# A transformer block on one core: the first queries and keys projected in parts, dense products in single pieces

## The chip, the cores and the metric

The kernel runs on one core of a Trainium2 chip. The metric is the device time of one execution in microseconds (us). Five engines work side by side, each on its own list of instructions, and wait for one another by semaphores: PE (matrix products, weights loaded beside them as PEld), DVE (vector), ACT (scalar functions), POOL (GpSimd) and SP, which here only issues DMAs. ACT can issue DMAs too. In a profile, L749 is line 749 of the kernel.

## The reference

```python
x = A_x                                     # 1 x 2048 x 512, bf16
h = x + attention(layernorm(x))             # 32 heads of 16; softmax over 2048 keys, then @ wo
h2 = h + (gelu(n @ w_gate) * (n @ w_up)) @ w_down     # n = layernorm(h); F = 1792
```

The scores of a head are (q . k) / 4; their softmax takes the maximum over all 2048 keys before the exponential.

## The kernel before, in words

**Scheduling.** The kernel is written by a planner in Python (class `Plan`). It keeps a clock for each engine, guesses when each operand is ready (`SEM`: a semaphore's delay; `pe_at`: the gap when PE changes its mode; `mm`: a product's length), and writes the instructions out in the order that its main loop finds. Only the order and the waits reach the chip; the guesses don't.

**Units and rows.** The 2048 queries are cut into 12 groups (four of 256, eight of 128), the 32 heads into 8 slots of four heads. A unit is one group with one slot: 96 units. A unit's first pass takes the row maxima: for each 512 keys, each 128 queries and each pair of heads, PE writes two banks of scores (L746) and DVE reduces them (L749, 128 x 1024 values). That is a "row"; there are 1024. Two pairs of banks alternate, so PE can be two rows ahead of DVE. Partial maxima are joined on POOL (L783, L784), or by a small reduction on DVE in the 128-wide groups (L808), split in three bf16 parts (L800 to L803), turned by a transposing DMA on SP (L823) and added to the queries on POOL (L828) in spare rows of the head's 32.

The second pass computes scores transposed, keys on partitions (L895), with the maximum already subtracted; ACT takes the exponential of 512 columns at a time (L904; 2048 of them, 32 for a unit of 256 queries, 16 for one of 128) into 34 tiles named PTM, PTE and PTG. PE multiplies them with the values (L926, a ones column giving the sums). Then come normalising (L960), the output projection, the second layer norm and the gated layer: gate and up (L1143), down (L1171), with GELU steps on POOL and ACT.

**PE's modes.** Scores are "rows" in the planner (32-row tiles of the array, mode `r`). All else is "dense": pieces of 0.22 us in the planner's clock, four to an item such as a projection, up to 56 products for a part of the gated layer. A change between the two waits for the products under way. The main loop picks a row or a dense piece. Coming from rows it may turn to dense work if ACT has enough queued (`LATE`) or the banks are not free; once there, it goes on while `nd`, the time spent since, is under 0.43, or while the piece would end ahead of both deadlines `D1` (DVE's) and `D2` (ACT's). Where PE would be idle, it multiplies a tile of ones (L452, "dummy") so that the array stays busy; `WARM` is the activity of the last 2.8 us under which that is forced.

**The head.** SP loads four x tiles of 128 tokens one by one (L470), then x tiles 4 to 7 (L473), the key weights and the query weights (L477), x tiles 8 to 11 and 12 to 15, the value weights, and wo (L484), each of 512 KB. DVE takes each tile's mean and variance (`ln_stats`, L503 and L504) and adds eps (L507), POOL the inverse root (L508), DVE normalises (`ln_norm`, L511), PE transposes (L538), ACT copies out (L540). After four tiles PE projects all 512 keys of the first chunk and then all 512 queries (L646) of the first 128 columns; ACT writes the keys (L675), DVE the queries (L671). A slot holds heads shifted by 16 partitions: odd slots come from a copy QKS (ACT, L680), moved by a DMA from SP (L687) into one of two QKS2 buffers and masked on POOL (L659). The statistics of tiles 4 to 7 are DVE's, ahead of the first row, and their normalising is POOL's (`ln_chain`, L521 to L531). Tiles 8 to 15 have their sums taken on ACT (`late_stats`, L1387), two passes a tile, and are normalised on POOL.

**Queues.** The first 32 rows belong to units 0 and 1 in an order by chunks of keys, and can be exchanged when keys are late. Key projections of the later chunks and the transposes stand in a list served first (`prio`); the other projections stand behind (`ready_q`), and both need a free QKS and QKS2 buffer (`can_projT`). POOL's work is a list with priorities (`jobs`), ACT's extra work another (`act_jobs`).

Of the kernel before, what the change touches and what calls it, by code (L numbers as in the profile page):

```python
# [19 lines left out]
class Plan:  # L20

    ENGINES = ("pe", "act", "dve", "pool", "sp")
    SEM = 0.045
    INF = float("inf")
# [118 lines left out]
    def pe_at(self, mode, tile=0, dep=0.0):  # L143
        t = max(dep, self.pe_last + 0.004)
        if self.pe_mode is not None and mode != self.pe_mode:
            return max(t, self.pe_drain + 0.09)
        return max(t, self.pe_tile.get(tile, 0.0))

    def mm(self, fn, reads=(), writes=(), n=512, mode="f", tile=0, sig=False, slow=1, extra=()):
# [8 lines left out]
        run = slow * n / (2400.0 if t > 4.8 else 1200.0) + 0.0025  # L158
# [103 lines left out]
def bass_sequential_preLN__mha_block__geglu_ffn__prompt_kernel(nc, A_x, A_wqkv, A_wo, B_x, B_w_gate, B_w_up, B_w_down, out):  # L262
    with ExitStack() as es:
# [175 lines left out]
        def run_act_jobs(now, force=False):  # L439
# [3 lines left out]
            for k, (fn, reads, writes) in enumerate(act_jobs):  # L443
                r = P.ready("act", reads, writes)
                if r <= max(a.free, now) + 0.02 and ((a.free <= now + 0.9) if force else (exps[0] - last_extra[0] >= 2)):
# [30 lines left out]
        def load_w(i, nm, lat):  # L476
            P.dma("sp", lambda e: e.dma_start(out=wqkv_sb[:, :, i * D:i * D + D], in_=wv[:, :, i * D:i * D + D]), nm, writes=[nm], lat=lat)  # L477
# [24 lines left out]
        def ln_stats(t):  # L502
            dve(lambda e: e.bn_stats(out=stats[:, t, :], in_=x_sb[:, t, :]), [("x", t)], [("stats", t)], 0.694, 0.672)  # L503
            dve(lambda e: e.bn_aggr(out=mv[:, t, :], in_=stats[:, t, :]), [("stats", t)], [("mv", t)], 0.1, 0.193)  # L504
# [5 lines left out]
        def ln_norm(t):  # L510
            dve(lambda e: e.tensor_scalar(out=xn_sb[:, t, :], in0=x_sb[:, t, :], scalar1=mv[:, t, 0:1], scalar2=rstd[:, t:t + 1], op0=ALU.subtract, op1=ALU.mult),  # L511
                [("x", t), ("rstd", t), ("mv", t)], [("xn", t)], 0.33, 0.43)

        def ln_chain(c, have_mv):
# [15 lines left out]
            for t in ts:  # L530
                ops.append(o(lambda e, t=t: e.tensor_scalar(out=xn_sb[:, t, :], in0=x_sb[:, t, :], scalar1=rstd[:, t:t + 1], scalar2=nmr1[:, t:t + 1], op0=ALU.mult, op1=ALU.add),  # L531
# [74 lines left out]
        def qkv_finished():  # L606
            qkv_over[0] = True
            fk = [("xnT", t) for t in range(NT)] + ["wk", "wq", "wv"] + [("QKS", i_) for i_ in range(4)] + [("QKS2", i_) for i_ in range(2)]
# [23 lines left out]
        def can_projT(it):  # L632
            return not (qks_busy.get(("a", qk_n[0] % 4)) or qks_busy.get(("b", qk_n[0] % 2)))

        def item_projT(it, which, ht, c):
            nm = "w" + which
# [17 lines left out]
            def mask(src, key, slot, bk):  # L654
# [9 lines left out]
                jobs.add(1, [(fn, [key, "qmask", "kmask", "kbias", "zero1"], keys, 0.74, 0.78, ())], then=over)  # L664
# [70 lines left out]
        def p1_issue():  # L735
# [18 lines left out]
            p1_on[0] = True  # L754
            nq = nq_of(gi)
# [252 lines left out]
        def add_ffn(gi):  # L1008
# [4 lines left out]
            fs = [list(range(a, min(NFC, a + nf))) for a in range(0, NFC, nf)]  # L1013
            for f, fcs in enumerate(fs):
                add_item(item_gate, gi, f, fcs, can=lambda i_, f=f: not par_busy[f % 2])
                add_item(item_up, gi, f, fcs)
            for k in range(nq_of(gi)):
                add_item(item_down, gi, k, can=lambda i_: not gut_left.get(gi, 0))
# [343 lines left out]
        for t in range(4):  # L1362
# [3 lines left out]
        def run_now(fn, b, *a):  # L1366
            it = Item(fn, a)
            it.b = b
            it.begin()
            try:  # L1370
                while True:
                    fill(P.ready("pe", it.req[1]), 7)
                    it.req = next(it.gen)
            except StopIteration:
                pass
# [204 lines left out]
```

## Time and profile before

| what | value |
|---|---|
| median of 3 runs | 1245.37 us |
| lowest, highest | 1240.93, 1245.42 us |
| the profiled execution's own time | 1243.96 us |
| its span, first to last instruction | 1242.2 us |
| mean granted TensorE clock | 0.990 |
| DVE busy, ACT busy, PE busy | 1194.4, 1196.1, 1170.5 us |
| POOL busy | 802.3 us |
| first row's maximum starts | 13.61 us |
| last row's maximum starts | 1203.05 us |

The profile is of one execution; times in it count from the span's start. A group's line gives the source line, the engine and operation, what it writes and reads, how many there are, then the busy time in us and the mean of one in ns, then the engine's idle time just ahead of them and what ended most of it. In a timeline row the first two numbers are the start and the length (merged rows cover several instructions), and the bracket gives the idle time before it and who ended it. In a table by stage, the stretch comes first, then its length, each engine's busy time and count, the granted clock and the DMA share. Busy time counts overlapping instructions once, so an engine with pipelined instructions can be busy throughout and still have room: for that the distance from start to start is the better measure.

### The profile page before, as it was taken

How to read it: one execution, taken by the hardware profiler on the slowest of the kernel's cores; microseconds unless marked ns; L12 is line 12 of the kernel's file. 1: busy time of each engine (PE TensorE's matmuls, PEld its weight loads, DVE VectorE, ACT ScalarE, POOL GpSimd, SP SyncE). 2: the span in 40 equal slices, each digit the busy share in tenths (PEclk: the TensorE clock that was granted, in tenths of full speed). 3: DMA queues.
4: the chain of work that ended last, by engine and by line, in shares of the span. 5: the costliest groups of instructions: out<-in, count | busy, mean ns of one | idle time of the engine just before them, and what ended most of it. 6: DMA issues, size and time to landing. Idle time of an engine off the chain costs nothing.

```text
span 1242.2 us, 39638 instructions
## 1 busy us (share of the span) xinstructions
PE 1170.5 (94%) x16858; PEld 612.4 (49%) x16997; DVE 1194.4 (96%) x1145; ACT 1196.1 (96%) x2503; POOL 802.3 (65%) x1629
## 2 busy tenths in 40 slices
PE   9999999999999999999999999999999999999998
PEld 5333333344334443334355655565656565666566
DVE  7999999999999999999999999999999999999982
ACT  6699999999999999999999999999999999999995
POOL 7667533778546984678826787394948484768254
PEclk9999999999999999999999999999989998999999
DMA  5011410000011000100000000100000000010000
GB/s 158 24 36 35 142 61 22 14 6 4 10 27 12 6 6 12 27 11 5 5 22 20 18 10 7 22 11 20 10 18 6 15 15 14 11 18 6 19 15 10
DMA packets 52081, 28.25 MB, mean 23 GB/s; under 512 B 37184, under 2 KB 50880, under 8 KB 51904
## 3 DMA queue, kind: packets, MB, share of 16 engines
q1 hardware_dynamic: 51904, 25.71, 8.3%
q8 instruction: 133, 2.18, 0.7%
q14 instruction: 44, 0.36, 0.1%
HBM read 11.80 MB, written 2.10 MB: 11 GB/s over the span
## 4 chain that ended last, share of the span: by engine, by line
ACT 59%; PE 19%; DVE 16%; POOL 3%; issue 1%; DMA 1%; POOLq 0%; DVEq 0%; ACTq 0%
ACT PTM L904 36%; DVE PM L749 16%; ACT PTG L904 10%; ACT PTE L904 6%; PE pbank L895 5%; PE pbank L746 3%; PE pbank L926 2%; PE pbank L1171 2%; PE pbank L452 2%; ACT th_sb L1124 1%; PE pbank L646 1%; PE pbank L697 1%; ACT g_sb L576 1%; ACT u_sb L576 1%; ACT OA L576 1%
## 5 line engine op out<-in xcount | busy, mean ns | idle before, releaser
L749 DVE TENSOR_REDUCE PM<-pbank 128x2 f32<-128x1024 f32 x1024 | 1173.4, 1221 | 17.1 <-PE pbank L746 7.0
L904 ACT ACTIVATE PTM<-pbank 128x512 bf16<-128x512 f32 x1388 | 730.1, 669 | 7.2 <-PE pbank L895 4.6
L895 PE MATMUL pbank<-QT,KT 32*128 32x128 bf16 (+1 forms) x6144 | 607.0, 236 | 23.5 <-ACT PTM L904 3.0
L746 PE MATMUL pbank<-KT,QT 32*128 32x512 bf16 x2048 | 398.9, 387 | 18.4 <-DVE PM L749 9.2
L895 PEld LDWEIGHTS pbank<-QT,KT 32*128 32x128 bf16 x6144 | 302.9, 93 | 228.2 <-issue 77.6
L904 ACT ACTIVATE PTG<-pbank 128x512 bf16<-128x512 f32 x420 | 225.8, 656 | 1.9 <-PE pbank L895 1.2
L746 PEld LDWEIGHTS pbank<-KT,QT 32*128 32x128 bf16 x2048 | 96.6, 91 | 175.5 <-DVE PM L749 83.6
L452 PE MATMUL pbank<-ones_bf 128*128 128x512 bf16 (+1 forms) x499 | 143.8, 365 | 13.3 <-issue 3.9
L926 PE MATMUL pbank<-PTM,VA 128*17 128x128 bf16 (+1 forms) x4164 | 135.1, 240 | 2.4 <-ACT PTM L904 0.8
L904 ACT ACTIVATE PTE<-pbank 128x512 bf16<-128x512 f32 x240 | 133.3, 656 | 1.4 <-PE pbank L895 1.3
L960 POOL TENSOR_TENSOR LINV<-OAT,negone 128x4 f32<-128x4 f32 (+1 forms) x94 | 114.9, 1232 | 28.9 <-ACT OAT L576 27.7
L926 PEld LDWEIGHTS pbank<-PTM,VA 128*17 128x17 bf16 x4164 | 78.2, 91 | 35.4 <-issue 15.1
L828 POOL TENSOR_TENSOR QT<-QT,STG 128x128 bf16<-128x128 bf16 (+1 forms) x95 | 48.2, 508 | 54.4 <-DMA STG<-ST 53.7
L800 POOL CAST ST<-NEGM 128x4 bf16<-128x4 f32 (+1 forms) x95 | 19.7, 207 | 94.5 <-DVE NEGM L808 92.0
L452 PEld LDWEIGHTS pbank<-ones_bf 128*128 128x128 bf16 x585 | 43.8, 98 | 71.9 <-ACT PTM L904 25.9
L783 POOL TENSOR_TENSOR MX<-PM,MX 128x8 f32<-128x8 f32 x96 | 19.4, 202 | 87.1 <-DVE PM L749 84.1
L1143 PE MATMUL pbank<-hnT_l,wg_sb 128*128 128x128 bf16 (+1 forms) x616 | 67.7, 241 | 1.1 <-ACT PTM L904 0.4
L1143 PE MATMUL pbank<-hnT_l,wu_sb 128*128 128x128 bf16 (+1 forms) x616 | 68.3, 240 | 0.4 <-ACT PTM L904 0.2
L1126 POOL TENSOR_TENSOR th_sb<-th_sb,g_sb 128x512 f32<-128x512 f32 (+1 forms) x56 | 67.1, 1199 | 1.5
L1130 POOL TENSOR_TENSOR th_sb<-th_sb,g_sb 128x512 f32<-128x512 f32 (+1 forms) x56 | 67.1, 1200 | 1.3
L1114 POOL TENSOR_TENSOR GUT<-th_sb,u_sb 128x512 bf16<-128x512 f32 (+1 forms) x56 | 66.9, 1200 | 1.4
L1171 PE MATMUL pbank<-wd_sb,GUT 128*128 128x512 bf16 (+1 forms) x214 | 62.3, 379 | 3.4 <-issue 2.4
(146 smaller groups left out, 1113.1 us busy)
## 6 DMA issues: line engine op xcount, KB each, us to landing
QKS<-QKS SPq DMA_DIRECT2D x32, 112.0 KB, 2.2
xres<-in_A_x_dram SPq DMA_DIRECT2D x16, 128.0 KB, 2.3
out_dram<-out_sb SPq DMA_DIRECT2D x15, 128.0 KB, 1.7
wg_sb<-in_B_w_gate_dram SPq DMA_DIRECT2D x4, 448.0 KB, 5.6
wu_sb<-in_B_w_up_dram SPq DMA_DIRECT2D x4, 448.0 KB, 7.3
x_sb<-in_A_x_dram SPq DMA_DIRECT2D x3, 512.0 KB, 7.1
wqkv_sb<-in_A_wqkv_dram SPq DMA_DIRECT2D x3, 512.0 KB, 6.2
STG<-ST SPq DMA_TRANSPOSE x96, 2.3
```

The costliest lines, as they stand in the source:

```text
L452: P.mm(lambda e: e.matmul(pbank[:, b, 0:n], ones_bf[:, 0:128], ones_bf[:, 0:n], start=True, stop=True), reads=["ones_bf"], writes=[("pb", ...
L746: P.mm(lambda e, g=g, b=b0 + jj: e.matmul(pbank[:, b, :], QT[32 * g:32 * g + 32, c, slot, col:col + 128], KT[32 * g:32 * g + 32, slot, 512 ...
L749: dve(lambda e: e.tensor_reduce(out=PM[:, par, kc, qh, 2 * gp:2 * gp + 2], in_=pbank[:, b0:b0 + 2, :], axis=AX.X, op=ALU.max), [("pb", b0) ...
L895: P.mm(lambda e, kt=kt, i=i: e.matmul(pbank[:, b, w * i:w * i + w], KT[32 * g:32 * g + 32, slot, 128 * kt:128 * kt + 128], QT[32 * g:32 * ...
L904: act(lambda e: e.activation(out=PTt(pi), in_=pbank[:, b, :], func=ACT.Exp), [("pb", b)], [("PT", pi)], 512, lat=0.605, ivl=0.48, extra=dX)
L926: P.mm(lambda e, g=g, kt=kt, pi=pi, i=i: e.matmul(pbank[32 * g:32 * g + 17, b, 0:w], VA[:, kt, head(slot, g), :], PTt(pi)[:, w * i:w * i + ...
L960: inv = [((lambda e, a=a: e.tensor_tensor(out=LINV[:, par, a:a + hh], in0=oat[:, a:a + hh, 16], in1=negone[:, 0:hh], op=ALU.pow)), [("OAT" ...
L1114: jobs.add(3, [o(lambda e: e.tensor_tensor(out=o_ap, in0=shp(ts_), in1=shp(us), op=ALU.mult), [kt, ku], [("GUT", fc) for fc in fcs], 1.25, ...
L1126: o(lambda e: e.tensor_tensor(out=ts_, in0=ts_, in1=gs, op=ALU.mult), [kt, kg], [kt], 1.25)], then=second)
L1130: o(lambda e: e.tensor_tensor(out=ts_, in0=ts_, in1=gs, op=ALU.mult), [kt, kg], [kt], 1.25)], then=first)
L1143: P.mm(lambda e, dc=dc, fc=fc, i=i: e.matmul(pbank[:, it.b, w * i:w * i + w], wsb[:, dc, 128 * fc:128 * fc + 128], hT[:, dc, 0:w], start=( ...
L1171: P.mm(lambda e: e.matmul(pbank[:, b, 0:cols[1] - cols[0]], GUT[:, fc, 128 * k:128 * k + 128], wd_sb[:, fc, cols[0]:cols[1]], start=(fc == ...
```

## The change

- Planner's constants: a semaphore's delay, the gap at a change of mode and the length of products are set longer.
- The first 128 columns of the query and key weights are loaded by two DMAs of their own on ACT's queue, at the start; SP loads x tiles 4 to 15, then the value weights, then the rest of the key and query weights.
- Head: DVE takes the statistics of tiles 0 to 3 in a row; ACT normalises tiles 0 and 1 (POOL makes the product of mean and inverse root), DVE tiles 2 and 3. 256 queries are projected after two tiles and copied by DVE; 384 keys after three tiles (copied by ACT), the last 128 keys after the fourth (by DVE). The other 256 queries follow. Copies for the shift are taken in parts.
- Statistics of tile 4 and 5 stay ahead of the first row; tiles 6 and 7 have theirs after rows 0 and 1, and are normalised by DVE after rows 4 and 5 (`DNORM`); POOL normalises 4 and 5.
- Before the exponentials start, up to three ACT jobs can be placed in one turn of the main loop, with a shorter look ahead; values may be projected while up to four ACT jobs are left; other projections wait until no key projection of the first columns is left in `prio`; an item of low priority can be paused for one of high priority.
- Main loop: after one piece (`nd` under 0.2) PE goes back to rows unless the next piece ends ahead of both deadlines; from row 881 on the limit is 0.43 as before. Thresholds: WARM 1.7 (1.6), LATE 1.0 (1.1), 1.30 (1.20), ACT's margin in D2 0.47 (0.40), the margin of the next piece 0.1 (0.09).
- Items of the gated layer get a pacing test, `paced`, with PACEG = 0.

The core of the diff:

```diff
-    SEM = 0.045
+    SEM = 0.048
...
-            return max(t, self.pe_drain + 0.09)
+            return max(t, self.pe_drain + (0.096 if mode == "r" else 0.091))
...
-        run = slow * n / (2400.0 if t > 4.8 else 1200.0) + 0.0025
+        run = slow * n / (2400.0 if t > 4.8 else 1200.0) + (0.011 if mode == "r" else 0.008 if n >= 512 else 0.004)
...
+        load_w(0, "wq0", 4.0, 0, 128, "act")
+        load_w(1, "wk0", 4.3, 0, 128, "act")
         load_x(1, 4.1)
-        load_w(1, "wk", 5.1)
-        load_w(0, "wq", 6.1)
-        load_x(2, 7.1)
-        load_x(3, 8.1)
-        load_w(2, "wv", 9.1)
+        load_x(2, 5.1)
+        load_x(3, 6.1)
+        load_w(2, "wv", 7.1)
+        load_w(1, "wk", 7.9, 128, D)
+        load_w(0, "wq", 8.7, 128, D)
...
         def can_projT(it):
+            if it.args[:2] != ("k", 0) and any(i_.fn is item_projT for i_ in prio):
+                return False
...
-                jobs.add(1, [(fn, [key, "qmask", "kmask", "kbias", "zero1"], keys, 0.74, 0.78, ())], then=over)
+                jobs.add(1 if ht == 0 and which == "k" else 2, [(fn, [key, "qmask", "kmask", "kbias", "zero1"], keys, 0.74, 0.78, ())], then=over)
...
+            def paced(j):
+                return gi >= PACEG or p1_i[0] >= n0 + rows * j / tot or P.warmth(max(P.pe_last, clock[0]), 2.8) < COOL
...
+        PACE, PACEG, COOL = 0.7, 0, 1.7
...
-        ln_stats(0)
-        ln_rstd(0)
-        ln_stats(1)
-        ln_rstd(1)
         for t in range(4):
+            ln_stats(t)
+            ln_rstd(t)
+            if t < 2:
+                ln_nmr(t)
+        ln_norm_act(0)
+        ln_norm_act(1)
+        for t in (2, 3):
             ln_norm(t)
-            if t < 2:
-                ln_stats(t + 2)
-                ln_rstd(t + 2)
-        for t in range(4, 8):
-            ln_stats(t)
+        ln_stats(4)
...
-        run_now(item_projT, 4, "k", 0, 0)
-        run_now(item_projT, 5, "q", 0, 0)
-        ln_chain(1, True)
...
+        head_T(0)
+        head_T(1)
+        head_T(2)
+        head_mm("q", 6, 0, 256)
+        t_q = head_q(6, 0, 256, "dve")
+        ln_stats(5)
+        head_T(3)
+        head_mm("k", 4, 0, 384)
...
+        head_mm("k", 5, 384, 512)
...
+        head_mm("q", 7, 256, 512)
+        head_qks(0, 6, 0, 256, [t_q])
+        head_qks(1, 4, 0, 384)
+        tok = head_qks(1, 5, 384, 512, [t_k])
...
+        head_q(7, 256, 512, "act")
...
+        dve_stats(1, (0, 1))
+        for t, r in DNORM.items():
+            row_hooks.setdefault(r, []).append(lambda t=t: ln_norm(t))
...
-        WARM, HOT, LATE = 1.6, 0.8, 1.1
+        WARM, HOT, LATE = 1.7, 0.8, 1.0
...
-            D2 = max(f2, a_eng.free - 0.40)
+            D2 = max(f2, a_eng.free - 0.47)
...
-                if sd < INF and sd <= best_row + 0.4 and (nd < 0.43 or ed + 0.09 <= min(D1, D2)):
+                if sd < INF and sd <= best_row + 0.4 and (nd < (0.43 if p1_i[0] > 880 else 0.2) or ed + 0.1 <= min(D1, D2)):
```

The new functions, in short: `ln_norm_act` normalises on ACT (scale = inverse root, bias = -mean times it, made by `ln_nmr` on POOL), `head_T` transposes a tile and has ACT copy it out, `head_mm` projects a range of tokens by four products, `head_q` copies queries on DVE or ACT, `head_qks` takes the copy for the shift, `head_shift` issues it on SP and masks on POOL, `dve_stats` puts statistics on DVE after given rows.

More of the change, by code (lines that the diff above doesn't have):

```diff
@@ L754, in p1_issue @@
             p1_on[0] = True
+            for fn_ in row_hooks.pop(n, ()):
+                fn_()
             nq = nq_of(gi)
@@ new lines, in head_q @@
+        def head_q(b, c0, c1, eng):
+            keys = [("qT", 0, t) for t in range(c0 // 128, c1 // 128)]
+            if eng == "dve":
+                return dve(lambda e: e.tensor_scalar(out=QT[:, 0, 0, c0:c1], in0=pbank[:, b, 0:c1 - c0], scalar1=qmask[:, 0:1], scalar2=None, op0=ALU.mult), [("pb", b), "qmask"], keys, 0.33, 0.43)
+            else:
+                act(lambda e: e.activation(out=QT[:, 0, 0, c0:c1], in_=pbank[:, b, 0:c1 - c0], func=ACT.Copy, scale=qmask[:, 0:1]), [("pb", b), "qmask"], keys, c1 - c0, lat=0.5, ivl=0.4)
@@ new lines, in head_qks, with head_shift, over @@
+        def head_qks(si, b, c0, c1, extra=()):
+            keys = [("QKSp", si, c0)] + ([("QKS", si)] if c1 == 512 else [])
+            return act(lambda e: e.activation(out=QKS[:, si, c0:c1], in_=pbank[:, b, 0:c1 - c0], func=ACT.Copy), [("pb", b)], keys, c1 - c0, extra=extra)
+        def head_shift(si, c0, o_ap, keys, s1, s2_):
+            P.dma("sp", lambda e: e.dma_start(out=QKS2[0:112, si, :], in_=QKS[16:128, si, :]), ("qks", si), reads=[("QKS", si), ("QKSp", si, 0), ("QKSp", si, c0)], writes=[("QKS2", si)], lat=2.2)
+            def over(t):
+                qks_busy[("a", si)] = qks_busy[("b", si)] = False
+                qkv_check()
+            jobs.add(1, [(lambda e: e.tensor_scalar(out=o_ap, in0=QKS2[:, si, :], scalar1=s1[:, 0:1], scalar2=s2_[:, 0:1], op0=ALU.mult, op1=ALU.add),
+                          [("QKS2", si), "qmask", "kmask", "kbias", "zero1"], keys, 0.74, 0.78, ())], then=over)
```

104 lines of the change are left out of this document (73 added, 31 removed).

## The prediction

> **What bounds the kernel now.** I read the engine sums first, then the costliest groups, then the sums by stage, then the timeline of the first 60 us.
>
> ```profile
> PE 1170.5 (94%) x16858; PEld 612.4 (49%) x16997; DVE 1194.4 (96%) x1145; ACT 1196.1 (96%) x2503; POOL 802.3 (65%) x1629
> ...
> L749 DVE TENSOR_REDUCE PM<-pbank 128x2 f32<-128x1024 f32 x1024 | 1173.4, 1221 | 17.1 <-PE pbank L746 7.0
> L904 ACT ACTIVATE PTM<-pbank 128x512 bf16<-128x512 f32 x1388 | 730.1, 669 | 7.2 <-PE pbank L895 4.6
> ...
> L452 PE MATMUL pbank<-ones_bf 128*128 128x512 bf16 (+1 forms) x499 | 143.8, 365 | 13.3 <-issue 3.9
> ```
>
> Three engines look full, but not alike. The maxima ("rows", L749) start every 1.131 us when nothing holds them up (the median from start to start), so 1024 take 1158.1 us. The exponentials (L904) start every 0.478 us, and with every other ACT operation at its own usual spacing ACT needs some 1090 of the 1145 us from 60 to 1205. PE holds 143.8 us of filler matmuls (L452). So DVE is the bound and ACT follows it with about 5% to spare. Counting rows against exponentials agrees: two exponentials belong to a row, and ACT is 70 behind at 100 us, 50 at 600, 33 at 1200, which is about one unit of work: it has caught up and waits for rows. The time is therefore: start of the first row + 1158.1 + what DVE loses between rows + what follows the last row.
>
> ```profile
> core 0: us, PE busy (x) PEld busy (x) DVE busy (x) ACT busy (x) POOL busy (x), PEclk, DMA share, GB/s
> 12.00:60.00 48.00, 46.89 (x302) 20.95 (x304) 41.62 (x38) 34.58 (x77) 35.74 (x78) 1.00 0.17 51
> 60.00:1038.00 978.00, 924.32 (x13065) 461.62 (x13178) 971.37 (x895) 969.35 (x2022) 647.44 (x1332) 0.99 0.08 20
> 1038.00:1204.00 166.00, 156.34 (x2905) 101.51 (x2927) 161.67 (x157) 163.07 (x351) 95.05 (x181) 0.98 0.06 13
> 1204.00:1242.20 38.20, 32.29 (x559) 23.52 (x550) 11.09 (x31) 24.82 (x51) 18.76 (x23) 0.95 0.06 13
> ```
>
> DVE is idle mostly in the head. By the starts of rows: row 0 at 13.61, row 32 at 55.73, row 880 at 1033.06, the last at 1203.05. Less 1.131 a row, and 0.087 (start to start) for each of the small maxima of the 128-wide groups, DVE loses **5.9** us up to row 32, **14.2** up to row 880, **6.7** after it. The last row ends at 1204.28, and 37.9 us of tail follow.
>
> ```profile
> 8.46 0.41 DVE L511 TENSOR_SCALAR xn_sb<-x_sb,mv,rstd 128x512 bf16<-128x512 bf16 x1 [0.44 <-POOL rstd L508]
> ...
> 11.42 0.78 ACT L675 ACTIVATE KT<-pbank,kbias,kmask 128x512 bf16<-128x512 f32 x1 [1.21 <-PE pbank L646]
> ...
> 12.28 0.75 DVE L671 TENSOR_SCALAR QT<-pbank,qmask 128x512 bf16<-128x512 f32 x1 [0.21 <-PE pbank L646]
> ...
> 13.61 4.62 DVE L749 TENSOR_REDUCE PM<-pbank 128x2 f32<-128x1024 f32 x4 [0.57 <-PE pbank L746]
> ...
> 19.28 4.62 DVE L749 TENSOR_REDUCE PM<-pbank 128x2 f32<-128x1024 f32 x4 [1.05 <-PE pbank L746]
> ```
>
> The first row waits for a chain: fourth tile normalised, transposed, all 512 keys projected, all 512 queries projected, queries copied out. Then the rows starve four times (1.05, 1.14, 2.54, 0.51 us) because keys come late.
>
> **The head, step by step.** (a) Statistics of tiles 0 to 3 follow each other at the 1.01 us seen between the first two (2.93, 3.94): tile 3 starts at 5.96 instead of 6.60. Its inverse root on POOL (0.65) ends near 7.8, also behind the two small new POOL products (0.25 each), so its normalising starts at 7.9 instead of 8.46. (b) Tiles 0 and 1 go to ACT (nearest row: the 0.62 of L1387, same shape from SBUF), near 5.1 and 6.1, and their copies of transposes queue behind; that is done by 7.9, before tile 2's. (c) 256 queries: projected near 8.0 to 8.5, copied out by DVE behind the statistics of tile 4 (8.3 to 9.1), so at 9.1 to 9.5, then tile 5 until 10.35. (d) Tile 3 transposed at 8.4, out of PSUM at 9.5; 384 keys projected beside that, out on ACT at 9.55 to 10.2; the last 128 keys projected by 9.9 and copied by DVE behind tile 5 at 10.35 to 10.55. The first row's matmul took 0.43 to its maximum (13.18, 13.61): first row at **11.1**.
>
> Loads: two new 128-column pieces of weights go out on ACT's queue (SP's issues take 0.40 to 0.51 each, so ACT's table load moves from 0.78 to about 1.7, and ACT is first needed at 5.1). They bring 256 KB ahead of or among the four x tiles, which landed at 2.90, 3.30, 3.94, 4.39 against uses at 2.93, 3.94, 5, 6. Bounds: nothing (they land behind) and 0.75 (a later 512 KB load took 1.5 us from landing to landing). I take 0.2, because only tile 0 has no slack: first row at **11.3, so -2.3** (-2.7 to -1.6). The big loads keep their sum on SP, x before weights, which helps. [...]
>
> (e) Added between rows: statistics of tiles 6 and 7 (0.80 each, the spacing of 8.79, 9.60) and two normalisings (0.41 each): **+2.4** on DVE, nothing hides them unless DVE would idle. What is queued behind them is the next row. (f) Starving: the second unit's keys and queries start their shift over SP near 11.8 instead of 12.7, and POOL isn't busy with four 0.77 us normalisings when they land, so row 4 isn't late: -1.05. Rows 4 to 7 end at 22.8 with the additions; tile 7 normalised at 20.5, transposed and copied by 21.7, second 512 keys out by 23.7, so row 8 at 24.1: 1.35 idle (before 1.14). Afterwards the key projections no longer queue behind other projections holding the shift buffers (before, such a projection ran at 17.23 and the keys waited until 22.35), and the later statistics are taken into ACT earlier: of 2.54 + 0.51 I leave 1.0. With 0.15 for small gaps 2.5 stays of 5.9: **-3.4** (0 to -5). Cover that can fail: weights for the second quarter now land last and start after the keys, near 35 us; unit 2 needs them at row 32, 52 us. Head in sum: -2.3 + 2.4 - 3.4 = **-3.3**; row 32 at 52.4.
>
> **Single pieces and new constants.** Out of row mode, PE may now issue one 0.22 us piece, and a second only if DVE's and ACT's backlog allow it, up to row 880; before, two were always allowed. In the trace, 852 such visits lie between 60 and 1204 us: 163 under 0.40 us (one piece, typically 0.32), 488 of 0.40 to 0.62 (two, 0.54), 201 longer. The row delays right behind them sum to 0.6, 9.1 and 6.3 us, with 3.5 behind none. So 79% of the 14.2 us up to row 880, 11.2 us, comes from long visits, and a short visit costs 0.0035 against 0.022. DVE has up to two rows in its two bank pairs when PE leaves, so I let half of the second pieces stay: 11.2 x 0.5 x 0.84 = **-4.7** (bounds -11.2, and a loss, the slower rival). The planner's new latencies, thresholds and the wider ACT margin only order the work; no row prices them: 0, bounds 5 either way (the waits at half clock, below). The pacing test is true for every group (its limit is group 0): nothing. After row 880 two pieces stay allowed, and the tail has its old code: 0.
>
> Sum: 1243.96 - 3.3 - 4.7 = **1236.0** by the profiled execution (span 1242.2 and 1.8 around it). The runs have the median 1245.37 and go from 1240.93, so the profiled one lies between them; I keep 1236.0.
>
> **Rivals.**
> - *Head only* (1240.7): DVE's waits come from the meeting of three engines and not from the length of a visit; -3.3 stays and the middle doesn't move. For it: 3.5 us lie behind no visit, and 4.9 of the waits stand in stretches at half clock. Against: the steep ratio of 0.022 to 0.0035.
> - *Nearly all goes* (1226.5): -3.3, all 11.2 and, by the planner's better latencies, a third of the last 6.7. For it: the waits are short (19 for L895, the longest 0.8), such as a planner errs by.
> - *PE runs out of room* (1254.7, slower). A split pair costs 0.64 instead of 0.54, and up to 0.1 more for the way in (0.15 to 0.21 from the last row matmul's start). About 560 pairs stand before row 880. Half split at 0.15 is 42 us, and the fillers there (111.5 us) cover that even if only every second one is movable. From about 75% split at 0.2 it is 84 us against 56: up to 28 short, then the products of exponentials and values fall behind, the 34 exponential tiles stay full, and ACT and then DVE stop. Half of 28, since second pieces return when nothing else is ready: 1243.96 - 3.3 + 14. Against: a third of the visits up to 600 us are fillers alone.
> - *No effect in sum* (1244): the head's lead is eaten by row 32 (late weights), the second pieces are nearly always allowed.
>
> The clock bears on all of them. It is halved in five stretches from 204 to 1044 us (20.5 us in all), in which DVE loses 4.9, although PE is busy 3.5 to 4.0 of 4 us there. So the raised filler threshold may remove up to 4.9, and shorter visits may add as much; I take 0. [...]
>
> **Numbers.** Forecast 0.40 (own range 1230 to 1240); head only 0.22; nearly all 0.18; PE 0.17; no effect 0.03. About 0.5%, 6.2 us, is what a measurement can tell from no change: under 1239.1 is faster, over 1251.6 slower. Faster 0.36 + 0.18 = 0.54, same 0.04 + 0.22 + 0.03 = 0.29, slower 0.17. Range 1222 to 1255: from the second rival less the constants' bound to the third.
>
> **What would show it.** First row at 11.3; gaps of rows after 8 and 12; row 32 at 52.4; loss up to row 880 near 9.5; fewer visits over 0.4 us and fewer L452. Wrong if the first row comes after 12, if row 32 lies past 54.5, or if ACT shows long waits for L895 between 300 and 1000 us.

## The result and the profile after

| | before | after |
|---|---|---|
| median of 11 runs each | 1241.79 us | 1261.51 us |
| lowest, highest | 1239.55, 1245.42 | 1248.26, 1273.18 |
| ratio, 95% interval | | 1.0116 [1.0085, 1.0146] |
| the profiled execution | 1243.96 | 1261.51 |
| its span, mean granted clock | 1242.2, 0.990 | 1259.8, 0.970 |
| row 0, row 32 | 13.61, 55.73 | 13.34, 55.36 |
| row 880, last row | 1033.06, 1203.05 | 1044.92, 1208.28 |
| from the last row's start to the end | 39.2 | 51.5 |

The change made the kernel slower. The ratios, here and below, leave out runs over 1.5% above the fastest of the same kernel (four of the eleven after); by their clock these belong with the rest, so the medians, 1.6% apart here, say more than the ratio. The spans differ by 17.6 us: -0.3 at row 0, -0.1 from there to row 32, **+12.2 from row 32 to row 880**, -6.6 from there to the last row, **+12.3 in the tail**. The last two belong together, as will be seen: from row 880 to the end the change takes 5.7 us more.

The profile's page after, engine sums, granted clock by slices of 31.5 us, and three groups (line 766 holds the maxima, 914 the transposed scores, 923 the exponentials):

```profile
PE 1195.5 (95%) x16643; PEld 610.5 (48%) x16750; DVE 1198.1 (95%) x1153; ACT 1195.9 (95%) x2501; POOL 802.6 (64%) x1629
...
PEclk9999999999999999999999899699999599999999
...
L766 DVE TENSOR_REDUCE PM<-pbank 128x2 f32<-128x1024 f32 x1024 | 1171.2, 1222 | 22.8 <-PE pbank L914 15.1
L923 ACT ACTIVATE PTM<-pbank 128x512 bf16<-128x512 f32 x1388 | 741.2, 692 | 17.5 <-PE pbank L914 13.2
...
L452 PE MATMUL pbank<-ones_bf 128*128 128x512 bf16 (+1 forms) x282 | 87.8, 371 | 7.9 <-ACT PTM L923 2.0
```

The sums look like those of before: the maxima take 1171.2 us against 1173.4. Three things moved. The filler matmuls went from 143.8 to 87.8 us. DVE's idle time ahead of the maxima grew from 17.1 to 22.8, most of it behind scores transposed, and ACT's ahead of the exponentials from 7.2 to 17.5. And the clock row has an 8, a 6 and a 5. The table by stage shows what lies there (columns as in the prediction's table):

```profile
core 0: us, PE busy (x) PEld busy (x) DVE busy (x) ACT busy (x) POOL busy (x), PEclk, DMA share, GB/s
708.00:719.00 11.00, 10.64 (x142) 6.07 (x141) 8.61 (x9) 9.25 (x19) 9.46 (x14) 0.53 0.12 31
797.00:822.00 25.00, 23.59 (x292) 13.12 (x295) 19.84 (x19) 20.23 (x38) 4.46 (x13) 0.52 0.08 20
822.00:971.00 149.00, 141.66 (x2644) 91.69 (x2651) 147.34 (x146) 146.57 (x318) 95.35 (x191) 1.00 0.06 13
971.00:1010.00 39.00, 38.49 (x605) 24.90 (x603) 32.43 (x31) 32.83 (x66) 22.00 (x52) 0.52 0.04 8
1045.00:1208.00 163.00, 155.07 (x2891) 100.65 (x2909) 163.00 (x161) 159.86 (x342) 112.73 (x210) 1.00 0.07 17
1208.00:1260.00 52.00, 42.81 (x776) 31.84 (x774) 16.60 (x39) 36.38 (x74) 26.86 (x31) 0.97 0.04 10
```

Three stretches ran at half clock, 10.2, 23.9 and 37.5 us of them (75.1 us in the whole execution, against 24.2 before); each is a multiple of the 3.41 us that most stretches of before lasted, 3, 7 and 11 times. DVE is idle for 2.4, 5.2 and 6.6 us in these windows, and for 1.7 in the 149 us between them. PE is busy for 94 to 99% of each: it works, but slower (a row's product, L763, takes 577 ns on average from 797 to 822 and 384 from 822 to 971). In the 3.4 us ahead of each it was busy for 96, 97 and 91%, without a filler. By the starts of rows DVE lost 26.6 us from row 32 to the last one (21.0 before), 17.9 of it in half clock (4.6 before): outside half clock the change loses less, 8.7 against 16.4. Up to row 880 alone it is 17.9 in half clock (2.1 before) and 8.6 outside (12.3 before), so the half clock is more than the whole +12.2 of that stretch. From row 881 on, where the old limit of two pieces holds, DVE is busy without a gap. In the tail ACT and PE work off what was left: the last exponential starts 31.9 us behind the last row (19.4 before), and 19.7 us follow its start (19.8 before). At row 880 the exponentials had been level (1728 started, 1723 before).

The eleven runs of this one program show the same. Those at a clock of 0.990, 0.982, 0.970 and 0.957 took 1248.26, 1254.70, 1261.51 and 1270.15 us: -6.8 us for +0.01 of clock (r = -0.98 over all eleven). The runs of before (clock 0.988 to 0.997, median 0.993) give -7.8. Of the 20 us between the medians about 15.6 go with the clock (0.993 to 0.970 at 6.8 per 0.01), and some 5.5 stay at equal clock (1249.1 against 1243.6, each read at 0.99 from a line through the kernel's own runs; the two shares are read separately and don't add up exactly). The profiled pair agrees: 0.990 to 0.970 is 13.6 us at that price, and DVE lost 13.3 us more in half clock (17.9 against 4.6). "At 0.99" below means such a reading; with few runs it is good to a few us only.

### The profile page after: what moved, and what is told of

Read it like the earlier page. It is cut to its first block, busy times and chain, and to the rows that moved or that the text cites. A ratio compares the mean times of both kernels' runs of the same rounds, so it can differ in the third digit from the quotient of the medians.

```text
span 1259.8 us, 39157 instructions
## 1 busy us (share of the span) xinstructions
PE 1195.5 (95%) x16643; PEld 610.5 (48%) x16750; DVE 1198.1 (95%) x1153; ACT 1195.9 (95%) x2501; POOL 802.6 (64%) x1629
## 4 chain that ended last, share of the span: by engine, by line
ACT 49%; DVE 27%; PE 12%; POOL 9%; issue 2%; DMA 2%; POOLq 0%; DVEq 0%; ACTq 0%
ACT PTM L923 28%; DVE PM L766 26%; ACT PTG L923 9%; ACT PTE L923 5%; PE pbank L914 5%; PE pbank L945 2%; PE pbank L763 2%; ACT th_sb L1149 1%; PE pbank L1168 1%; DMA STG<-ST 1%; ACT QKS L697 1%; ACT g_sb L590 1%; PE pbank L1196 1%; ACT u_sb L590 1%; POOL LINV L979 1%
## 5 line engine op out<-in xcount | busy, mean ns | idle before, releaser
L766 DVE TENSOR_REDUCE PM<-pbank 128x2 f32<-128x1024 f32 x1024 | 1171.2, 1222 | 22.8 <-PE pbank L914 15.1
L923 ACT ACTIVATE PTM<-pbank 128x512 bf16<-128x512 f32 x1388 | 741.2, 692 | 17.5 <-PE pbank L914 13.2
L914 PE MATMUL pbank<-QT,KT 32*128 32x128 bf16 (+1 forms) x6144 | 665.9, 240 | 24.3 <-ACT PTM L923 6.2
L914 PEld LDWEIGHTS pbank<-QT,KT 32*128 32x128 bf16 x6144 | 321.2, 94 | 231.6 <-ACT PTM L923 85.9
L763 PE MATMUL pbank<-KT,QT 32*128 32x512 bf16 x2048 | 407.5, 394 | 16.2 <-DVE PM L766 5.5
L763 PEld LDWEIGHTS pbank<-KT,QT 32*128 32x128 bf16 x2048 | 97.1, 91 | 153.0 <-DVE PM L766 74.0
L945 PE MATMUL pbank<-PTM,VA 128*17 128x128 bf16 (+1 forms) x4164 | 153.6, 244 | 2.7 <-ACT PTM L923 1.4
L452 PE MATMUL pbank<-ones_bf 128*128 128x512 bf16 (+1 forms) x282 | 87.8, 371 | 7.9 <-ACT PTM L923 2.0
L1168 PE MATMUL pbank<-hnT_l,wu_sb 128*128 128x128 bf16 (+1 forms) x616 | 75.8, 247 | 1.0 <-ACT PTM L923 0.7
L1168 PE MATMUL pbank<-hnT_l,wg_sb 128*128 128x128 bf16 (+1 forms) x616 | 75.4, 246 | 1.3 <-issue 0.3
L1196 PE MATMUL pbank<-wd_sb,GUT 128*128 128x512 bf16 (+1 forms) x211 | 69.0, 382 | 1.8 <-issue 1.0
L1153 POOL TENSOR_TENSOR th_sb<-g_sb 128x512 f32<-128x512 f32 (+1 forms) x56 | 55.2, 986 | 23.9 <-ACT g_sb L590 21.1
```

The lines of the kernel that those rows point to most:

```text
L452: P.mm(lambda e: e.matmul(pbank[:, b, 0:n], ones_bf[:, 0:128], ones_bf[:, 0:n], start=True, stop=True), reads=["ones_bf"], writes=[("pb", ...
L763: P.mm(lambda e, g=g, b=b0 + jj: e.matmul(pbank[:, b, :], QT[32 * g:32 * g + 32, c, slot, col:col + 128], KT[32 * g:32 * g + 32, slot, 512 ...
L766: dve(lambda e: e.tensor_reduce(out=PM[:, par, kc, qh, 2 * gp:2 * gp + 2], in_=pbank[:, b0:b0 + 2, :], axis=AX.X, op=ALU.max), [("pb", b0) ...
L914: P.mm(lambda e, kt=kt, i=i: e.matmul(pbank[:, b, w * i:w * i + w], KT[32 * g:32 * g + 32, slot, 128 * kt:128 * kt + 128], QT[32 * g:32 * ...
L923: act(lambda e: e.activation(out=PTt(pi), in_=pbank[:, b, :], func=ACT.Exp), [("pb", b)], [("PT", pi)], 512, lat=0.605, ivl=0.48, extra=dX)
L945: P.mm(lambda e, g=g, kt=kt, pi=pi, i=i: e.matmul(pbank[32 * g:32 * g + 17, b, 0:w], VA[:, kt, head(slot, g), :], PTt(pi)[:, w * i:w * i + ...
```

## The experiments

"Loss" is what DVE lost from row 32 to the last row, by the starts of rows as in the prediction; in brackets how much of it lies in half-clock stretches (before 21.0 [4.6], after 26.6 [17.9]). "Fillers" are counted by their weight loads (before 585, after 330; some matmul records are missing from the groups above). "Left" is how many of the 2048 exponentials had not started at the last row (before 35, after 56). These counts come from the one profiled execution of a kernel, whose clock can differ from the median one that is given (0.982 for the head alone, 0.981 for more fillers, 0.967 for the old delays).

**Two pieces again.** The change with its main edit undone:

```diff
-... (nd < (0.43 if p1_i[0] > 880 else 0.2) or ed + 0.1 <= min(D1, D2)):
+... (nd < 0.43 or ed + 0.1 <= min(D1, D2)):
```

> The changed kernel with two dense pieces allowed again for all rows (limit of nd 0.43), all else as changed. Theory A (single pieces take the place of the filler matmuls, the array is less active, its clock is halved for tens of us, and rows wait there): fillers (L452) back from 282 towards 499, half-clock time from 75 us to under 30, row 32 to row 880 from 989.6 back to about 978, time near 1243. Theory B (the changes of mode use up PE's time, the clock follows): also near 1243, but with fillers and waits by mode, so this run alone does not part A from B. Theory C (the planner's new constants and thresholds are the cause, not the single pieces): stays over 1255.

1266.16 us, 1.0214 [1.0196, 1.0232], at clock 0.994. Loss 8.1 [1.8], under half of that before, and yet slower than the change. The table by stage of this kernel:

```profile
60.00:1025.00 965.00, 933.57 (x12648) 444.89 (x12646) 961.71 (x890) 947.66 (x1943) 642.54 (x1320) 1.00 0.08 20
1025.00:1190.00 165.00, 158.15 (x2940) 96.91 (x2939) 164.31 (x164) 161.72 (x342) 89.96 (x178) 1.00 0.07 15
1190.00:1264.00 74.00, 67.04 (x1212) 44.72 (x1210) 18.64 (x47) 59.86 (x122) 30.97 (x39) 0.98 0.05 10
```

Rows run almost without a gap at full clock and end 13 us earlier than before; then 74 us of tail follow, with ACT busy for 60. 105 exponentials were left, 70 more than before: 34.5 us of tail for 70, **0.49 us each** (an exponential starts every 0.478 us). So single pieces are not the only cause: something else in the change holds ACT back, and single pieces mend that in part while they cost clock.

**Single pieces alone.** The kernel before with that one edit:

```diff
-... (nd < 0.43 or ed + 0.09 <= min(D1, D2)):
+... (nd < (0.43 if p1_i[0] > 880 else 0.2) or ed + 0.09 <= min(D1, D2)):
```

> The kernel before with nothing but the limit of nd at 0.2 up to row 880. Theory A: fillers fall under 350, half-clock time over 40 us, time 1250 to 1262, and the runs spread with the granted clock by about 6.8 us for each 0.01. Theory C: under 1247. Either way the head is that of before: first row at 13.6, row 32 near 55.7.

1257.89 us, 1.014 [1.0112, 1.0168], clock 0.982, 1251.7 at 0.99. Loss 28.6 [10.4], 33 left. The edit forecast at -4.7 costs 17.0 alone: about 8.6 by the clock (0.011 at 7.8 per 0.01) and 8 at equal clock. Outside half clock the loss is 18.2 against 16.4. The fillers were 554, not under 350 as expected. And the visits to dense work hardly became shorter: between rows 32 and 880, 564 of 809 last over 0.4 us, before 600 of 741, in the change 298 of 917. In that kernel a second piece is mostly taken all the same, so this run alone is a weak test of the pieces; the pairs with the new thresholds, below, are a better one.

**The values' ones later.** The change, with POOL's four memsets of the values' ones column made to wait for the first keys:

```diff
-  jobs.add(3, [(lambda e, a=a: e.memset(VA[...], 1.0), [], [("VO", a // 4)], ...
+  jobs.add(3, [(lambda e, a=a: e.memset(VA[...], 1.0), [("kT", 0, 0)], [("VO", a // 4)], ...
```

> The changed kernel; POOL's four memsets of the ones columns additionally wait for the first 512 keys, so that they don't run from 8.1 to 10.4 us beside DVE's normalising of tile 3. If DVE's 2.33 us there (0.41 for the other tiles) come from POOL working at the same time, it falls to 0.41 and the first row starts at 11.4 instead of 13.34. Rival: the 2.33 us come from the DMA traffic into x at that time (342 to 375 GB/s): then it stays over 2 and the first row at 13.3. The total follows by at most 1.9 us and drowns in the spread of the clock.

The first row came at 11.74 instead of 13.34. Here the timeline of the change, then of this kernel:

```profile
8.10 1.19 POOL L770 MEMSET VA<- 128x128 bf16 x2
...
8.18 2.33 DVE L513 TENSOR_SCALAR xn_sb<-x_sb,mv,rstd 128x512 bf16<-128x512 bf16 x1 [0.44 <-POOL rstd L510]
```

```profile
8.07 0.41 DVE L513 TENSOR_SCALAR xn_sb<-x_sb,mv,rstd 128x512 bf16<-128x512 bf16 x1 [0.44 <-POOL rstd L510]
```

The same normalising took 2.33 us beside POOL's memsets and 0.41 without them; it ended at 10.51, just behind the fourth memset (10.36). Row 8 did not come earlier, though: 27.21 against 27.24. Total 1265.43, 1.0191 [1.0166, 1.0215], at clock 0.968; a difference to the change isn't readable at such a spread of clocks.

**The head alone.** The change with all constants, limits and thresholds of before.

> The changed kernel with the planner's constants, the two pieces and the thresholds of before: the new head, the loads and the queues' rules alone. Theory A and C: the middle as before (row 32 to row 880 in about 977), head better by 0.3, time 1241 to 1244. If the new head itself slows the middle (by another order of projections), over 1248.

1244.67 us, 1.0033 [1.0021, 1.0045], clock 0.990. Row 32 at 55.83: the new head gains nothing there. It is 3.8 us slower than the kernel before beside it (1240.86, clock 0.993), of which some 2.3 go with the clock. Loss 28.7 [13.2], 33 left; outside half clock that is 15.5, about as before.

**More fillers.** Both filler thresholds raised in the change:

```diff
-        WARM, HOT, LATE = 1.7, 0.8, 1.0
+        WARM, HOT, LATE = 2.1, 0.8, 1.0
...
-... (heat < 1.30 and ed + 0.31 <= D1)):
+... (heat < 1.70 and ed + 0.31 <= D1)):
```

> The changed kernel with the filler threshold WARM at 2.1 (1.7) and the heat test at 1.70 (1.30): more filler matmuls, single pieces kept. Clock theory: mean clock from 0.970 to over 0.985, half-clock time from 75 us to under 35, and the time at least 8 us under the changed kernel's 1261.5. Room theory (PE has no time left, the fillers that went were the reserve): exponentials fall further behind the rows, time equal or higher than 1261.5 although the clock rises.

1278.87 us, 1.0295 [1.0268, 1.0322], clock 0.989. Loss 16.6 and a last row 10.6 us earlier than in the change, but 130 exponentials left and a tail of 84.9. The clock came back and the time didn't: with 533 fillers instead of 330 the exponentials fall behind (1650 started at row 880 instead of 1728). That the clock explains everything falls with this.

**The clock by itself.** Both thresholds lowered in the kernel before, so fewer fillers and nothing of the change:

```diff
-        WARM, HOT, LATE = 1.6, 0.8, 1.1
+        WARM, HOT, LATE = 1.0, 0.8, 1.1
...
-... (heat < 1.20 and ed + 0.31 <= D1)):
+... (heat < 0.60 and ed + 0.31 <= D1)):
```

> The kernel before with WARM at 1.0 (1.6) and the heat test at 0.60 (1.20), two pieces kept: fewer filler matmuls and nothing else changed by intent. Clock theory: fillers under 400, clock under 0.98, half-clock time over 60 us and time 6.8 us up for each 0.01 of clock, so over 1249. Room theory: fewer fillers are more room, time 1241 or less.

1321.15 us, 1.0632 [1.06, 1.0664], clock 0.870. Page of this kernel:

```profile
PEclk9999776798877888777999798998999897798898
...
L749 DVE TENSOR_REDUCE PM<-pbank 128x2 f32<-128x1024 f32 x1024 | 1182.6, 1215 | 84.5 <-PE pbank L895 61.4
```

The clock is down in most slices from the fifth on, 345 us at half clock in all. Of 98.1 us that DVE loses behind row 32, 80.5 lie there; the tail is the old one (38.1). That is the first mechanism almost alone: fewer fillers, lower clock, rows late. It had 359 fillers (by their weight loads), and the change 330 at a clock of 0.970: the number of fillers is not the whole rule.

**Which constants hold ACT back.** Four kernels with the new head and two pieces. With the old delays and old thresholds it is the head alone. One has the new delays and lengths (SEM, `pe_at`, `run`) with the old thresholds, one the reverse, and one both, but with the two filler thresholds old. In the diff's terms the halves are

```diff
+    SEM = 0.048
+            return max(t, self.pe_drain + (0.096 if mode == "r" else 0.091))
+        run = ... + (0.011 if mode == "r" else 0.008 if n >= 512 else 0.004)
```

```diff
+        WARM, HOT, LATE = 1.7, 0.8, 1.0
+            D2 = max(f2, a_eng.free - 0.47)
+... (heat < 1.30 and ed + 0.31 <= D1)):
```

> The new head with two pieces and the old thresholds (WARM, LATE, heat, margins), but the planner's new delays and lengths. With two pieces and all new constants ACT was 70 exponentials behind the kernel before at the last row, and the tail was 73.7 us. If the new delays and lengths do that: tail over 60 us, time over 1258. If the thresholds do it (earlier leaving of the rows, more fillers): tail under 45, time 1241 to 1248.

> The changed kernel with two pieces for all rows and only the two filler thresholds of before (WARM 1.6, heat 1.20). If the additional fillers (695 against 585) are what took PE's time from the exponentials: exponentials at the last row back over 1990, time under 1255. If the delays or LATE do it: still under 1970 at the last row and over 1260.

> The new head with two pieces, the planner's old delays and lengths and the new thresholds. At a clock of 0.99 the neighbours give 1245.1 (old delays, old thresholds), 1259.6 (new delays, old thresholds) and 1269.9 (both new). If the thresholds alone hold the exponentials back: under 1980 at the last row, 1254 to 1258 at 0.99. If they do harm only with the new delays: 2010 at the last row and under 1248.

| two pieces, new head | median us, ratio | clock | at 0.99 | loss | left |
|---|---|---|---|---|---|
| old delays, old thresholds | 1244.67, 1.0033 | 0.990 | 1245.1 | 28.7 [13.2] | 33 |
| new delays, old thresholds | 1291.62, 1.0398 | 0.940 | 1259.6 | 38.3 [32.9] | 74 |
| old delays, new thresholds | 1260.36, 1.0153 | 0.992 | 1262.4 | 10.5 [1.6] | 87 |
| both new, old filler thresholds | 1277.41, 1.0291 | 0.976 | 1266.9 | 24.4 [19.1] | 100 |
| both new (two pieces again, above) | 1266.16, 1.0214 | 0.994 | 1269.9 | 8.1 [1.8] | 105 |

Each half costs 14 to 17 us at equal clock, both together 25 (of the new delays' 14, 3.5 lie in the head: row 32 at 59.31 instead of 55.83). The row of the new thresholds is the clearest: full clock, DVE losing 10.5 us less than before, and 52 more exponentials left at the end, for 26.7 us of tail (65.9 against 39.2), 0.51 each. The last four rows and the kernel with more fillers (130 left) had all issued the same 1120 gate and up products at the last row; their tails go from 58.9 us (74 left) to 84.9, 0.46 for each exponential, and 19.5 to 20.7 us follow the start of the last one in each. So it is the exponentials that were left that set these tails. Of the thresholds, those of the fillers raise the clock (0.976 to 0.994) and save 11 us by it, for about 3 at equal clock; with them old, 100 exponentials are still left, so beside the new delays they are not what holds ACT back. LATE, D2's margin and the margin of the next piece were not tried alone: which of them holds ACT back stays open.

**The old delays in the whole change** (single pieces, new thresholds).

> The changed kernel with the planner's old delays and lengths, single pieces and new thresholds kept. With two pieces the new delays and lengths alone cost 14 us at equal clock and 0.05 of clock. If they act the same way with single pieces: better than the changed kernel, time under 1252. If they are needed by the single pieces (they make PE turn back to rows and exponentials earlier): 1260 or more.

1263.97 us, 1.0159 [1.012, 1.0197], clock 0.982, 1256.1 at 0.99, against 1249.1 with the new delays. With single pieces the new delays are worth some 7 us, at the limit of what four runs can tell; with two they cost 7 to 14 (by the table).

This kernel and the row "old delays, new thresholds" differ in the limit alone, and so do the change and "two pieces again". With the new thresholds the limit does shorten the visits: over 0.4 us last 316 of 942 here (710 of 868 with two pieces) and 298 of 917 in the change (704 of 849). The loss outside half clock between rows 32 and 880 goes up with it, from 7.7 to 12.4 and from 4.6 to 8.6, and before, with the pieces alone, from 12.3 to 15.0. With the limit at one piece the waits were longer, three times out of three.

**Single pieces to the end** (limit 0.2 for all rows).

> The changed kernel with single pieces for all rows, the last 143 too. In the changed kernel the tail grew from 39.2 to 51.5 us, because ACT had 1992 exponentials done at the last row instead of 2013; up to row 880 it was level (1728, 1723). If that comes from two pieces under the new constants after row 880: at the last row over 2005, tail under 45, and time at equal clock (0.99) near 1244 instead of 1249; the clock stays low. If it is the dense work put off until then (gate and up 784 of 1232 done at row 880, before 896): tail stays over 50 or grows.

1283.58 us, 1.0342 [1.0318, 1.0367], clock 0.962. Both signs came, one of each theory: only 35 exponentials are left, as before, and yet the tail grew to 65.7. The stage of the tail in this kernel:

```profile
1218.00:1284.00 66.00, 60.22 (x880) 47.57 (x882) 16.60 (x39) 30.91 (x62) 44.34 (x51) 1.00 0.04 10
```

ACT is busy for 31 us of it, PE for 60. The last exponential starts 19.4 us behind the last row, as before, but 46.2 us follow it instead of 19.8. At the last row 1032 of the 1232 gate and up products (L1168, without the 112 of the tail's own line) were issued (1133 in the change, 1184 before). In the change the products issued at row 880 are 784, against 896 before; the two pieces from row 881 on catch up a part, and there the exponentials fall behind instead. So dense work is put off, and its bill is the tail, in the one form or the other. Every kernel with single pieces and the new thresholds has 784 at row 880, single pieces alone have 896, and those with two pieces 828 or more: it takes both.

**Bulk loads later.** The second unit's shift is a small DMA on SP's queue behind the bulk loads. First the kernel before, with the loads of the value weights and wo issued behind the first two shifts; then the head alone with late ones and the bulk weights (rest of keys and queries, wo) behind them.

```diff
+        def late_loads():
+            load_w(1, "wk", 3.5, 128, D)
+            load_w(0, "wq", 4.5, 128, D)
...
+            if si == 0:
+                late_loads()
```

The call stands in `head_shift`, behind its DMA.

> The kernel before, with the loads of the value weights and wo issued behind the first two shifts instead of ahead of them. The first shifts were issued at 12.7 us and landed when the last bulk load did, near 16.4. Theory: they land at 15 or earlier, row 4 starts by 18.3 instead of 19.28, row 32 comes 1 to 2.5 us earlier than 55.73 and the time goes down by as much, to 1238 to 1240. Rival: a later event sets row 32 (POOL's normalising, the projections' order): under 0.5 us, time as before.

> The new head with the main loop and constants of before, the ones columns late, and the rest of the key and query weights and wo issued behind the first two shifts. With the ones late alone the first row came at 11.74, but row 8 stayed at 27.2 and row 32 at 55.3, because the shifts, issued at 11.6, landed at 16.6 with the last bulk load, and POOL's normalising of tiles 4 to 7 stands behind their masks. Theory: shifts land by 14.5, row 8 by 25.2, row 32 by 53.5, time 1241 to 1243. Rival: row 32 stays over 55.

In the kernel before it moved nothing: 1.001 [0.9998, 1.0023], row 4 at 19.11 (19.28), because POOL's four normalisings stand ahead of the mask until 17.0 anyway. In the new head it did: 1239.60 us, 0.9992 [0.9977, 1.0007], which is the same time as before, but with row 8 at 25.40 and row 32 at 53.97 (55.73 before). Timelines of the values' ones made late, then of this kernel:

```profile
11.59 1.25 SPq L1412 DMA_DIRECT2D QKS<-QKS  x2
...
16.70 0.76 POOL L1417 TENSOR_SCALAR KT<-QKS,kmask,kbias 128x512 bf16<-128x512 bf16 x1 [3.11 <-DMA QKS<-QKS]
```

```profile
14.47 0.76 POOL L1420 TENSOR_SCALAR KT<-QKS,kmask,kbias 128x512 bf16<-128x512 bf16 x1 [0.34 <-DMA QKS<-QKS]
...
25.40 18.21 DVE L767 TENSOR_REDUCE PM<-pbank 128x2 f32<-128x1024 f32 x16 [1.74 <-PE pbank L764]
```

Issued at 11.59 behind bulk loads that ran until 16.4, the shift landed at 16.6, and POOL sat idle for 3.11 us; issued at 12.13 with only the value weights still ahead (landed at 13.0), it landed at 14.4. POOL's normalising of tiles 4 and 5 stands behind the two masks, and row 8 behind it.

**Clock put back, two ways.** Single pieces alone with WARM 1.75; the new head with its late loads with WARM 1.7.

> The kernel before with single pieces up to row 880 and WARM at 1.75 (1.6). Clock theory alone: the clock rises from 0.982 to over 0.988 and the time falls from 1257.9 to under 1253. Room theory: the added fillers push exponentials back, the tail grows from 41.7 to over 46, and the time stays at 1257 or more although the clock rises.

> The best kernel so far (new head, ones columns and loads late, two pieces, constants and thresholds of before, 1239.6) with WARM at 1.7 (1.6). Clock theory: clock from 0.994 to 0.996 or more, time 1237 to 1239. Room theory: the exponentials fall behind, tail from 38.0 to over 41, time over 1241.

Single pieces with more fillers: 1251.05 us, 1.008 [1.0052, 1.0107], clock 0.994; the fillers returned 6.8 of the 17.0 us, and 8.7 at equal clock stay. New head with late loads: 1240.39 us against 1242.21, 0.9982 [0.9970, 0.9995], clock 0.994. That is 0.18% faster than the kernel before beside it, little more than that kernel's own median moves from one set of runs to the next (1240.71 to 1242.21, 0.12%). Without the higher threshold it had 1239.60 at the same clock of 0.994, so there was no clock to put back, and WARM gained nothing that can be read. In its profile row 32 is 1.5 us earlier than before and the loss 14.8 [1.7], so the last row comes 7.8 us earlier, at 1195.25; but 44 exponentials are left instead of 35, and the tail of 43.4 gives 4.2 back.

## Why the prediction was wrong, point by point

The step that failed is **single pieces and new constants**: -4.7 for the pieces, "0, bounds 5 either way" for the constants and the clock. Measured: +12.2 up to row 880 (+15.8 in half clock, -3.7 outside it), -6.6 behind it, +12.3 in the tail.

- *The pieces.* Long visits stood ahead of long waits, and I took them for the cause. Made single, with nothing else or in the two pairs with the new thresholds, the waits outside half clock grew, by 2.7 to 4.7 us up to row 880. The ratio 0.022 to 0.0035 was a correlation; that a long visit stands where PE has room may be the reason, but no run tests it. In the whole change these waits did shrink up to row 880, by 3.7, close to the forecast -4.7. That is luck: two pieces with the new constants have 4.6 there, so the constants shortened them and the pieces gave half of it back.
- *The clock.* I put it at 0, with 4.9 either way: I named the loss, but bounded it by what the half clock had cost before, and did not ask how much half clock the edit could add. It was the largest term, some 15 of 20 us, as a loss. The rows that could have said so were on the page: fillers alone in a third of the visits up to 600 us, and waits of 4.9 us in only 20.5 us of half clock, 0.24 us lost per us of it. By that ratio the 71.7 us between row 32 and the last row after give 17.2, and 17.9 were measured; the kernel before with lowered filler thresholds has 80.5 in 334, 0.24. What I missed is that an edit that leaves PE over 90% busy can still lower the clock: PE was 91 to 97% busy in the 3.4 us ahead of each stretch after, and the mean clock went from 0.990 to 0.970.
- *The constants.* "Only order the work" was true, and order was worth 14 to 25 us with two pieces. I had read ACT as having 5% to spare and catching up; so it seemed free. Each exponential that has not started at the last row costs 0.46 to 0.51 us, and the planner trades rows against exponentials. "What follows the last row" was a term of my sum with no forecast of its own; "the tail has its old code: 0" was wrong though the code is the same.
- *The slower rival* had the direction right and the price too low, 14 instead of 20. Dense work was put off, as it says (784 products at row 880), but the exponentials were level there and fell behind only after it: this part is the 5.7 us from row 880 to the end, the smaller one. The clock was not in it.
- *First row*, forecast 11.3, measured 13.34. The two missing terms: DVE's normalising of tile 3 beside POOL's memsets, +1.92, and x tile 0 landing at 3.27 instead of 2.90, +0.37, where I took 0.2. Without the memsets 11.74 was measured. The later x tiles slipped more than tile 0: tiles 1 to 3 by 0.94, 1.18 and 1.46, tiles 4 to 7 by 0.86; none of these but tile 0 set the first row of this execution. That only tile 0 has no slack was wrong all the same: in the head alone tile 2 landed at 5.90, and its statistics waited for it. Nine profiled kernels have this head with the early memsets, and their first rows lie between 13.34 and 15.45, those of the old head between 13.37 and 13.61: the change's own 13.34 is the best of nine, and -0.3 no gain.
- *Added DVE work*, +2.4: as forecast, by the spacing of rows 0 to 7.
- *Starving*, 5.9 to 2.5 forecast: measured 5.9 to 3.4. Row 8 came at 27.24, forecast 24.1, at 27.2 with either first row: "POOL isn't busy when they land" held, but the shifts were issued at 13.19, not 11.8, and landed at 16.5. The head in sum is -0.4 at row 32 instead of -3.3.
- *What would show it* worked as a test: first row past 12, row 32 past 54.5, loss up to row 880 at 26.6 instead of 9.5, and ACT's waits for transposed scores between 300 and 1000 us at 11.7 us (4.0 before). Fewer long visits (298 over 0.4 us between rows 32 and 880, 600 before) and fewer fillers came as named; the fillers were the bad sign, not the good one.

That the clock follows the filler thresholds is shown by the runs in both directions (lowered in the kernel before, 0.993 to 0.870; raised with single pieces, 0.982 to 0.994, and in the change, 0.970 to 0.989). The number of fillers doesn't settle it: 359 give 0.870 in one kernel and 330 give 0.970 in another, and 554 with single pieces alone give 0.982 where 551 in the head alone give 0.990. Why is open: single pieces spread the dense work, and that may be the reason for the first pair, but no run separates it.

## What to carry to other kernels

Filler work that keeps an engine's clock up is not spare room (359 fillers instead of 585, with the thresholds lowered in the kernel before: clock 0.870, 80 us more). Before costing an edit that removes it, ask what the clock was in the stretches that have little of it, and price one more microsecond of half clock (0.24 to 0.25 us of the bound engine here: 80.5 in 334 us with the thresholds lowered in the kernel before, 17.9 in 71.7 in the change). Where one stage is traded against another, forecast the work left at the end, by counting what has started at the last step of the bound engine; a bound engine that runs without gaps can still mean a slower kernel. A chain that is made earlier gains only as far as the next step in another queue, so follow it to the second and the eighth row, not to the first.

## What the hardware showed that was not expected

- One program's time went from 1248 to 1273 us, in step with its mean granted clock (0.990 to about 0.960). In the profiled execution, half-clock stretches of 10 to 38 us stand while PE is 94% busy or more. Before, a stretch was 3.4 us, or 6.8 once.
- A DVE normalising (128x512, bf16) beside four memsets on POOL took 2.33 us, and 0.41 with the memsets later. It started at 8.18, behind the start of the first memset (8.10), and ended at 10.51, behind the end of the fourth (10.36): what it lost, 1.92 us, lasted through several of POOL's instructions in a row. What the two engines share there, no run shows.
- A shift DMA on a queue with bulk loads ahead took 3.3 us from issue to landing in the change and 5.0 with the values' ones later, and 2.3 in the new head with most of the bulk loads issued behind it.
